# GpSimd's pattern shifts in six equivalent forms that take turns

## The chip, the cores and the metric

The kernel runs on one core of a Trainium2 chip. The metric is the device time of one execution in microseconds (us), lower is better. The engines are named as in the profile: PE is TensorE's matmul (PEld its weight load), ACT is ScalarE, DVE is VectorE, POOL is GpSimd, SP is SyncE. Each engine works through its own list of instructions in order; engines wait for each other on semaphores.

## The reference

Two attention blocks over a sequence of 2048 with width 512 and 32 heads of 16 channels, on separate inputs A and B. Their outputs stand side by side in `out` (2048 x 1024, bf16).

```python
# A: linear attention
pq, pk = phi(q), phi(k)          # phi(t) = (t + 1 if t > 0 else exp(t)) + 1e-6
o = (pq @ (pk^T v)) / (pq @ sum(pk) + 1e-6)      # per head
a = o @ wo
# B: softmax attention
scores = einsum("bhqd,bhkd->bhqk", q, k) * 16 ** -0.5
o = einsum("bhqk,bhkd->bhqd", softmax(scores), v)
b = o @ wo
return concatenate([a, b], axis=-1)
```

Nearly all of the time goes to B: 32 heads with a 2048 x 2048 table of exponentials each.

## The kernel before, in words

**Two ways to an exponential.** B is cut into 32 units: 4 groups of 8 heads, times 4 chunks of 512 queries, times the even or the odd heads of the group. A unit has 64 blocks: 16 key tiles of 128 for each of 4 heads. TensorE makes the scores of a block, 128 keys by 512 queries (line 871). Then the block goes one of two ways.

- On ScalarE: an exponential of two or three blocks at once, from PSUM to fp16 tiles in `PT` (line 1084). There are 648 of these.
- On VectorE and GpSimd: VectorE turns the scores into int16 numbers, `score * ESC + EB` (line 987). Read as fp16, such a bit pattern is a rough exponential (the linear interpolation between powers of two). To smooth the error, two more patterns are made from it by adding an integer: 328 and 656, the two entries of `SHIFT`. This is the "pattern shift". The three fp16 readings of one block all go into the weighted sum with V: the first through `VX` (V times the constant `VW`), the two shifted ones through `VV` (line 1253).

**The buffers.** `DI` holds 8 buffers (`NDG`) of up to two blocks (`DG`) each, in three versions: 0 the pattern, 1 shifted by 328, 2 shifted by 656. `di_at(v, b)` gives the place of version v of buffer b. A buffer comes free when TensorE has used all its versions.

**The shifts on GpSimd.** `chain` (line 1120) asks for both shifts when a buffer's patterns are complete. A shift normally goes to GpSimd (`on_pool`); version 2 goes to VectorE (`on_dve`, line 1141) where the planner's estimate of GpSimd's backlog is too long. Each buffer has one or two blocks, so a shift is 512 or 1024 elements wide in each of 128 partitions. Where two shifts wait together, `on_pool` joins them into one instruction over two buffers, twice as wide. Where one of the two is version 1 and the other version 2 ("mixed"), the second is made from version 1 by adding another 328, so one constant serves both. The instruction is the `tensor_scalar` at line 1176, with multiplication by 1.0 and then addition of the shift, int16 in and int16 out. There are 369 of them: 198 with 2048 elements a partition, 169 with 1024, 2 with 512.

**What sets the order.** A planner in the kernel's own host code simulates the engines with fixed durations, picks the next piece of work by due times and priorities (the table `SEG` changes these priorities every few us), and appends it to the engines' lists. It counts a GpSimd shift as 0.276 us and 0.83 ns an element. The order on each engine is therefore written out before the kernel runs and doesn't react to real durations; only the semaphore waits do. The planner counts the shift's duration, not its operations.

**Other work.** On GpSimd: zeros, ones and masks at the start (lines 485 to 522), `VX` from `VV` (line 684, `tensor_scalar` with two multiplications, bf16), and the normalisation of a unit's result (line 1288, `tensor_tensor`). Block A, the projections and the output products are jobs that the planner fills into TensorE and VectorE between the blocks of B.

Of the kernel before, what the change touches and what calls it, by code (L numbers as in the profile page):

```python
# [8 lines left out]
F32 = mybir.dt.float32  # L9
# [3 lines left out]
ALU = mybir.AluOpType  # L13
# [225 lines left out]
def bass_concat_heads__linear_attn_block__softmax_full_mha__prompt_kernel(nc, A_x, A_wqkv, A_wo, B_x, B_wqkv, B_wo, out):  # L239
# [19 lines left out]
    SHIFT = (328, 656)  # L259
# [98 lines left out]
    sch = Sched()  # L358
    es = contextlib.ExitStack()
    with es:  # L360
        block = es.enter_context(nc.Block())

        def sb(name, shape, dt):
            return es.enter_context(nc.sbuf_tensor(name, shape, dt))

        def ps(name, shape, dt):
            return es.enter_context(nc.psum_tensor(name, shape, dt))
# [12 lines left out]
        DI = sb("DI", [128, NDG * (32 + 2 * DGW + (DGW // 32) * 33 + 32)], I16)  # L380

        def di_at(v, b):

            if v == 0:
                return b * (32 + DGW) + 32
            if v == 1:
                return NDG * (32 + DGW) + b * DGW
            return NDG * (32 + 2 * DGW) + b * ((DGW // 32) * 33 + 32)
# [21 lines left out]
        TOP = sb("TOP", [128, 3], F32)  # L410
        TP1 = sb("TP1", [1, 4], F32)
        FLG = sb("FLG", [1, 1], F32)

        S5 = ps("pS", [128, 5 * 512], F32)
        SCR = [S5[:, 0:1024], S5[:, 1536:2560]]
# [18 lines left out]
        def gapped(ap, c0, n, run):  # L434

            base = ap[:, c0:c0 + run]
            return bass.AP(base.tensor, base.offset, [list(base.ap[0]), [run + 1, n], [1, run]])
# [70 lines left out]
        band(ZMk, 8, 1, "ZMk")  # L508
        sch.add("pool", lambda e: e.memset(DI[:, 0:NDG * (32 + DGW)].rearrange("p (b n) -> p b n", b=NDG)[:, :, 0:32], 0.0), writes=[("DI", 2, b_) for b_ in range(NDG)])
        sch.add("pool", lambda e: e.memset(EA[:, 512:528], 0.0), writes=["EA"])  # L510
        for e_ in range(2):
            sch.add("dve", lambda e, e_=e_: e.tensor_reduce(PAR[:, e_:e_ + 1], ZMk[:].rearrange("p (a e) -> p e a", e=2)[:, e_, :],
                                                           axis=AX.X, op=ALU.max),
                    reads=["ZMk"], writes=[("PAR", e_)])
# [24 lines left out]
        def push(eng, ready, prio, dur, run):  # L539
            seq[0] += 1  # L540
            c_ = (ready, prio, seq[0], dur, run)
            cands[eng].append(c_)
            return c_
# [32 lines left out]
        def f_op(lane, fn, reads=(), writes=()):  # L576
            return lambda bk: sch.add(lane, fn, reads=reads, writes=writes)
# [78 lines left out]
        def flag_job(**kw):  # L656
            def f(e, bk):
# [10 lines left out]
                ("pool", 0.15, f_op("pool", lambda e: e.tensor_tensor(TP1[:, 3:4], TP1[:, 3:4], TP1[:, 0:1], op=ALU.mult), ["TP1", "TP1b"], ["TP1b"])),  # L668
                ("pool", 0.15, f_op("pool", lambda e: e.tensor_tensor(FLG[:], TP1[:, 3:4], TP1[:, 2:3], op=ALU.mult), ["TP1", "TP1b"], ["FLG"]))],
                [("GRX", i) for i in range(4)] + [("TOP", 1), ("TOP", 2)], [], rel=2, **kw)  # L670
# [239 lines left out]
        def d_backlog(at):  # L910

            w = max(0.0, T["dve"] - at) + sum(c_[3] for c_ in cands["dve"])
            return w
# [206 lines left out]
        def chain(buf):  # L1120
            s_ = dgroup["st"][buf]
            if not s_["closed"] or len(s_["items"]) < s_["taken"]:
                return
            s_["chained"] = True
            late = left[NU - 1] < DE3 and all(b[0] == NU - 1 for b in s_["items"])
            n = len(s_["items"])
            w = 512 * n
            rk = [("DI", 0, buf, i) for i in range(n)]

            def give(buf_, v, lane, en_):  # L1130
                for i, b in enumerate(dgroup["st"][buf_]["items"]):
                    if lane == "dve":
                        P = gapped(DI.bitcast(F16), di_at(v, buf_) + 33 + i * 528, 16, 32)
                    else:
                        P = DI.bitcast(F16)[:, di_at(v, buf_) + i * 512:di_at(v, buf_) + (i + 1) * 512]
                    pv_ready[b[0]].append((en_ + (PM if lane == "pool" else LPE["dve"]), b, (P, ("DI", v, buf_)), ("d", buf_), "V"))

            def shift(v, t_):
                def on_dve(st_, en_):
                    wide = w + 32  # L1140
                    sch.add("dve", lambda e: e.tensor_scalar(gapped(DI, di_at(v, buf), wide // 32, 32), DI[:, di_at(0, buf) - 32:di_at(0, buf) + w], 1.0, float(SHIFT[v - 1]),  # L1141
                                                             op0=ALU.mult, op1=ALU.add), reads=rk, writes=[("DI", v, buf)])
                    give(buf, v, "dve", en_)

                def on_pool(st_, en_):
                    d1 = lambda b_: dgroup["st"][b_].get("v1", 1e9)
                    two = [x for x in pshift if x[2] == w and x[1] != buf and x[3][0] <= st_ + PMW
                           and (x[0] == v or d1(x[1] if v == 1 else buf) <= st_ + PMX)]
                    pshift.remove(me[0])
                    segs = [(buf, v)]  # L1150
                    keys = list(rk)
                    if two:
                        o = min(two, key=lambda x: (x[0] != v, x[3][2]))
                        pshift.remove(o)
                        cands["pool"].remove(o[3])
                        segs = sorted(segs + [(o[1], o[0])])
                        st_ = max(st_, o[3][0])
                        if o[0] != v:
                            st_ = max(st_, d1(o[1] if v == 1 else buf) - 0.03)
                            keys = []  # L1160
                            for b_, v_ in segs:
                                keys += [("DI", 1, b_)] if v_ == 2 else [("DI", 0, b_, i) for i in range(n)]
                        else:
                            keys += o[4]
                        T["pool"] = en_ = st_ + 0.276 + 2 * w * 0.00083
                    mixed = len({v_ for _, v_ in segs}) == 2
                    moves = sorted((di_at(1 if mixed and v_ == 2 else 0, b_), di_at(v_, b_)) for b_, v_ in segs)

                    def view(offs):
                        one = DI[:, offs[0]:offs[0] + w]  # L1170
                        if len(offs) == 1:
                            return one
                        return bass.AP(one.tensor, one.offset, [list(one.ap[0]), [offs[1] - offs[0], 2], [1, w]])
                    sv, dv = view([m_[0] for m_ in moves]), view([m_[1] for m_ in moves])
                    sh_ = float(SHIFT[0] if mixed else SHIFT[v - 1])
                    sch.add("pool", lambda e: e.tensor_scalar(dv, sv, 1.0, sh_, op0=ALU.mult, op1=ALU.add),  # L1176
                            reads=keys, writes=[("DI", v_, x) for x, v_ in segs])
                    for x, v_ in segs:
                        if v_ == 1:
                            dgroup["st"][x]["v1"] = en_  # L1180
                        pv_give[x, v_](en_)
                pv_give[buf, v] = lambda en_: give(buf, v, "pool", en_)
                if late:
                    def plain(st_, en_):
                        sch.add("dve", lambda e: e.tensor_scalar(DI[:, di_at(v, buf):di_at(v, buf) + w], DI[:, di_at(0, buf):di_at(0, buf) + w], 1.0, float(SHIFT[v - 1]), op0=ALU.mult, op1=ALU.add),
                                reads=rk, writes=[("DI", v, buf)])
                        give(buf, v, "plain", en_)
                    push("dve", t_, -2, 0.06 + w * 0.00027, plain)
                elif v == 2 and p_backlog(t_) - DSH * d_backlog(t_) > PSH:
                    push("dve", t_, 1, 0.06 + (w + 32) * 0.00053, on_dve)  # L1190
                else:
                    me = [(v, buf, w, push("pool", t_ + LAT + 0.05, 0, 0.276 + w * 0.00083, on_pool), rk)]
                    pshift.append(me[0])
            for v in (1, 2):
                shift(v, s_["t"])
# [178 lines left out]
        for t, bk, lane in ((2, SBANKS[1], "dve"), (3, SBANKS[2], "act")):  # L1374
            def tr(e, t=t, bk=bk):
# [6 lines left out]
                reads=[bk[3]], writes=[("xTb", t)])  # L1382
# [224 lines left out]

        flag_op = sch.last_write["FLG"]
        flag_op.sig = True
# [12 lines left out]
        def run(queue, e):  # L1622
            got = []
            def hook(e):
                e.wait_ge(sems[flag_op.lane], flag_op.count)
                got.append(e.value_load(FLG.bitcast(mybir.dt.int32)[0:1, 0:1], min_val=0))  # L1626
            sch.emit_queue(queue, e, sems, hook=(mark.idx - 1, hook))
# [54 lines left out]
```

## Time and profile before

| | |
|---|---|
| median of 2 runs | 661.57 us (661.22 to 661.92) |
| the profiled execution's own time | 660.98 us |
| its span in the trace | 659.2 us |
| mean granted TensorE clock | 0.999 |
| ScalarE busy | 644.7 us |
| TensorE busy | 633.3 us |
| VectorE busy | 632.1 us |
| GpSimd busy | 592.7 us, of it 554.4 us in the shifts of line 1176 |

How to read the lines that follow: a group's row names the line, the engine, the operation, output and inputs with their shapes, and the count; then the busy time in us and the mean of one in ns; then the idle time of that engine just before, and what ended most of it. A row of the waits gives the total in us, the number of waits and the longest. A row of the stretches gives, for each engine, the busy us and the number of instructions, then the granted clock, the share of the DMA engines and GB/s. A row of the order in time gives start, length, engine, line and the instructions joined in it. GpSimd's spans are rough.

### The profile page before, as it was taken

How to read it: one execution, taken by the hardware profiler on the slowest of the kernel's cores; microseconds unless marked ns; L12 is line 12 of the kernel's file. 1: busy time of each engine (PE TensorE's matmuls, PEld its weight loads, DVE VectorE, ACT ScalarE, POOL GpSimd, SP SyncE). 2: the span in 40 equal slices, each digit the busy share in tenths (PEclk: the TensorE clock that was granted, in tenths of full speed). 3: DMA queues.
4: the chain of work that ended last, by engine and by line, in shares of the span. 5: the costliest groups of instructions: out<-in, count | busy, mean ns of one | idle time of the engine just before them, and what ended most of it. 6: DMA issues, size and time to landing. Idle time of an engine off the chain costs nothing.

```text
span 659.2 us, 15950 instructions
## 1 busy us (share of the span) xinstructions
PE 633.3 (96%) x6609; PEld 200.4 (30%) x6662; DVE 632.1 (96%) x1089; ACT 644.7 (98%) x686; POOL 592.7 (90%) x450
## 2 busy tenths in 40 slices
PE   8999999999999999999999999999999999999997
PEld 6323333222333333332222233322222223232222
DVE  4999999999999999999999999999999999999995
ACT  6999999999999999999999999999999999999994
POOL 5999999999999999999998899999999999999983
PEclk9999999999999999999999999999999999999999
DMA  9701010020102101210012011010011000120102
GB/s 178 207 3 33 1 34 6 11 43 9 34 2 33 21 14 33 65 34 9 9 27 64 17 34 34 18 19 10 7 26 41 17 1 11 25 26 25 33 26 67
DMA packets 53213, 21.53 MB, mean 33 GB/s; under 512 B 44177, under 2 KB 52625, under 8 KB 53137
## 3 DMA queue, kind: packets, MB, share of 16 engines
q1 hardware_dynamic: 51664, 19.80, 13.9%
q8 instruction: 54, 0.88, 0.6%
q10 hardware_dynamic: 1472, 0.66, 0.4%
q14 instruction: 23, 0.18, 0.1%
HBM read 4.46 MB, written 4.19 MB: 13 GB/s over the span
## 4 chain that ended last, share of the span: by engine, by line
ACT 96%; PE 3%; DMA 1%; ACTq 0%; issue 0%; DVE 0%; DVEq 0%
ACT PT L1084 93%; ACT EA L693 2%; DMA Wb<-in_B_wqkv_dram 1%; PE pPV L1253 1%; PE pD L809 1%; PE pS L871 0%; PE pD L1305 0%; PE pS L1305 0%; PE pS L1389 0%; ACTq L442 0%; PE pD L1389 0%; DVE KNa L582 0%; PE pD L659 0%; PE pD L871 0%; DVEq L1626 0%
## 5 line engine op out<-in xcount | busy, mean ns | idle before, releaser
L1084 ACT ACTIVATE PT<-pS 128x1024 f16<-128x1024 f32 (+1 forms) x648 | 636.6, 1305 | 1.0 <-PE pS L871 1.0
L1176 POOL TENSOR_SCALAR DI<-DI 128x2048 int16<-128x2048 int16 (+1 forms) x369 | 554.4, 1503 | 47.3 <-DVE DI L987 20.2
L987 DVE TENSOR_SCALAR DI<-pD 128x512 int16<-128x512 f32 x492 | 324.4, 679 | 6.1 <-PE pD L871 2.5
L871 PE MATMUL pS<-QT,KM 32*128 32x512 bf16 x1556 | 255.0, 384 | 8.8 <-ACT PT L1084 4.5
L1253 PE MATMUL pPV<-PT,VV 128*17 128x512 f16 x1369 | 233.7, 381 | 0.0
L1253 PE MATMUL pPV<-DI,VV 128*17 128x512 f16 x1358 | 227.3, 382 | 0.0
L871 PE MATMUL pD<-QT,KM 32*128 32x512 bf16 x492 | 170.5, 384 | 0.3 <-DVE PQT L696 0.3
L1253 PE MATMUL pPV<-DI,VX 128*17 128x512 f16 x679 | 161.0, 381 | 0.2 <-DVE OT L1282 0.2
L871 PEld LDWEIGHTS pS<-QT,KM 32*128 32x128 bf16 x1556 | 64.6, 91 | 265.3 <-ACT PT L1084 227.4
L987 DVE TENSOR_SCALAR DI<-pS 128x512 int16<-128x512 f32 x187 | 126.6, 677 | 0.7
L1141 DVE TENSOR_SCALAR DI<-DI 128x1056 int16<-128x1056 int16 x113 | 77.0, 687 | 0.5
L1253 PEld LDWEIGHTS pPV<-PT,VV 128*17 128x17 bf16 x1369 | 47.5, 88 | 41.4 <-issue 36.1
L1253 PEld LDWEIGHTS pPV<-DI,VV 128*17 128x17 bf16 x1358 | 47.0, 88 | 40.4 <-issue 33.0
L871 PEld LDWEIGHTS pD<-QT,KM 32*128 32x128 bf16 x492 | 40.5, 91 | 5.4 <-DVE DI L987 2.0
L1253 PEld LDWEIGHTS pPV<-DI,VX 128*17 128x17 bf16 x679 | 34.2, 88 | 22.0 <-issue 17.7
L718 PE MATMUL pD<-Wa,xTa 128*128 128x256 bf16 x200 | 30.5, 275 | 0.3 <-DVE DI L987 0.2
L600 PE MATMUL pD<-xTb,Wb 128*128 128x512 bf16 x67 | 21.2, 383 | 3.1 <-issue 2.3
L1282 DVE STREAM_TRANSPOSE OT<-pPV 128x512 f32<-128x512 f32 x31 | 21.9, 705 | 0.1
L582 DVE CAST KNa<-pD 128x512 bf16<-128x512 f32 x27 | 18.4, 681 | 3.0 <-PE pD L809 2.0
L1288 POOL TENSOR_TENSOR OT<-OT,ZR 128x256 bf16<-128x256 f32 x31 | 19.3, 621 | 1.6
L718 PEld LDWEIGHTS pD<-Wa,xTa 128*128 128x128 bf16 x200 | 15.4, 97 | 13.3 <-issue 6.3
L693 ACT ACTIVATE EA<-pD 128x512 bf16<-128x512 f32 x23 | 19.2, 835 | 0.0
(136 smaller groups left out, 346.3 us busy)
## 6 DMA issues: line engine op xcount, KB each, us to landing
out_dram<-KNa SPq DMA_DIRECT2D x31, 128.0 KB, 1.7
Wa<-in_A_wqkv_dram SPq DMA_DIRECT2D x1, 1536.0 KB, 8.2
KM<-KR SPq DMA_DIRECT2D x96, 16.0 KB, 1.8
Wb<-in_B_wqkv_dram SPq DMA_DIRECT2D x2, 384.0 KB, 4.5
Wb<-in_B_wqkv_dram SPq DMA_DIRECT2D x1, 512.0 KB, 4.6
Wa<-in_A_wo_dram SPq DMA_DIRECT2D x1, 512.0 KB, 4.5
Wa<-in_B_wo_dram SPq DMA_DIRECT2D x1, 512.0 KB, 3.7
ON<-in_B_x_dram ACTq DMA_DIRECT2D x1, 256.0 KB, 3.1
```

Source lines behind the costliest of these rows:

```text
L582: return lambda e, bk: (e.tensor_copy(out_fn(), in_fn(bk)) if lane == "dve" else e.activation(out_fn(), in_fn(bk), ACTF.Copy))
L600: return e.matmul(f32v(bk), lhsT=Wb[:, cc, kind * 512 + Gp * 128:kind * 512 + Gp * 128 + 128], rhs=xTb[:, cc, sc * 512:(sc + 1) * 512], st ...
L693: ("act", 0.052 + n * 0.000833, f_ev("act", lambda e, bk: e.activation(EA[:, 0:n], f32v(bk)[:, c0:c0 + n], ACTF.Exp), [], ["EA"])),
L718: return e.matmul(f32v(bk)[:, 256 * tt:256 * tt + 256], lhsT=xTa[:, b, cc, (o + tt) * 128:(o + tt + 1) * 128], rhs=Wa[:, cc, 512 * kind + ...
L871: return e.matmul(dst, lhsT=KM[32 * g:32 * g + 32, Gp % 2, e_, j * 128:(j + 1) * 128], rhs=QT[32 * g:32 * g + 32, Gp % 2, c * 512:(c + 1) ...
L987: sch.add("dve", lambda e: e.tensor_scalar(DI[:, di_at(0, buf) + i * 512:di_at(0, buf) + (i + n) * 512], f32v(DBANK[b0], n * 512), ESC, EB ...
L1084: sch.add("act", lambda e: e.activation(PTf[:, p0 * 512:p0 * 512 + w], S5[:, c0:c0 + w], ACTF.Exp, scale=SC), reads=skeys(sl, len(bl)), wr ...
L1141: sch.add("dve", lambda e: e.tensor_scalar(gapped(DI, di_at(v, buf), wide // 32, 32), DI[:, di_at(0, buf) - 32:di_at(0, buf) + w], 1.0, fl ...
L1176: sch.add("pool", lambda e: e.tensor_scalar(dv, sv, 1.0, sh_, op0=ALU.mult, op1=ALU.add), reads=keys, writes=[("DI", v_, x) for x, v_ in s ...
L1253: sch.add("pe", lambda e, g=g, j=j, c0=c0, V_=V_, r2=r2, P=P, first=first, last_=last_: e.matmul(PVb[32 * g:32 * g + 17, 0:512] if len(P.s ...
L1282: sch.add("dve", lambda e: e.transpose(OT[:, 0, :], PVb[:, 0:512]), reads=[("PV", g) for g in range(4)], writes=[("OT", 0)])
L1288: ("pool", 0.7, f_op("pool", lambda e: e.tensor_tensor(xn[:, :, 16 * e_:16 * e_ + 16], o[:, :, 0:16], zr.unsqueeze(2).broadcast_to([128, 1 ...
```

## The change

Six ways to write the same shift take turns. A counter for each pair of constant (328 or 656) and number of buffers (one or two) picks the form, so each form gets close to a sixth of the instructions of each kind. The integers involved are exact in every form. Form 0 is the old instruction. Form 5 takes the constant from a new tile in SBUF, `SHC` (two columns of 128 partitions), which GpSimd fills with two memsets at the start, ahead of the zeros of `KM`. Operands, order, declared reads and writes and the planner's durations stay as they were.

```diff
+        SHC = sb("SHC", [128, 2], F32)
+        nform = defaultdict(int)
...
+        for v_ in range(2):
+            sch.add("pool", lambda e, v_=v_: e.memset(SHC[:, v_:v_ + 1], float(SHIFT[v_])), writes=["SHC"])
...
                     sh_ = float(SHIFT[0] if mixed else SHIFT[v - 1])
-                    sch.add("pool", lambda e: e.tensor_scalar(dv, sv, 1.0, sh_, op0=ALU.mult, op1=ALU.add),
-                            reads=keys, writes=[("DI", v_, x) for x, v_ in segs])
+                    kind_ = (sh_, len(segs))
+                    form = nform[kind_] % 6
+                    nform[kind_] += 1
+
+                    def op(e):
+                        if form == 0:
+                            return e.tensor_scalar(dv, sv, 1.0, sh_, op0=ALU.mult, op1=ALU.add)
+                        if form == 1:
+                            return e.tensor_scalar(dv, sv, sh_, 1.0, op0=ALU.add, op1=ALU.mult)
+                        if form == 2:
+                            return e.tensor_scalar(dv, sv, sh_, None, op0=ALU.add)
+                        if form == 3:
+                            return e.tensor_scalar(dv, sv, -sh_, None, op0=ALU.subtract)
+                        if form == 4:
+                            return e.tensor_scalar(dv, sv, sh_ / 2, sh_ / 2, op0=ALU.add, op1=ALU.add)
+                        return e.tensor_scalar(dv, sv, SHC[:, int(sh_ == SHIFT[1]):int(sh_ == SHIFT[1]) + 1], None, op0=ALU.add)
+                    sch.add("pool", op, reads=keys, writes=[("DI", v_, x) for x, v_ in segs])
```

## The prediction

> **What bounds the kernel now.** The profiled execution took 660.98 us, with a span of 659.2 us and some 1.7 us around it; it lies 0.6 us (0.1%) under the median of the runs shown, 661.57 us. All sums below are made against the profiled execution. I read the busy shares first, then the chain of work that ended last, then the costliest groups.
>
> ```profile
> PE 633.3 (96%) x6609; PEld 200.4 (30%) x6662; DVE 632.1 (96%) x1089; ACT 644.7 (98%) x686; POOL 592.7 (90%) x450
> ...
> ACT 96%; PE 3%; DMA 1%; ACTq 0%; issue 0%; DVE 0%; DVEq 0%
> ...
> L1084 ACT ACTIVATE PT<-pS 128x1024 f16<-128x1024 f32 (+1 forms) x648 | 636.6, 1305 | 1.0 <-PE pS L871 1.0
> L1176 POOL TENSOR_SCALAR DI<-DI 128x2048 int16<-128x2048 int16 (+1 forms) x369 | 554.4, 1503 | 47.3 <-DVE DI L987 20.2
> ```
>
> ScalarE bounds it: it makes 96% of the chain, and in front of its 648 exponentials it stood idle for 1.0 us in all. GpSimd is nowhere in the chain. Its busy share of 90% looks like 10% of room, and that is the figure to be careful with, because the edit touches 369 of its 450 instructions. So I went on to the stretches and to GpSimd's order in time.
>
> ```profile
> core 0: us, PE busy (x) PEld busy (x) DVE busy (x) ACT busy (x) POOL busy (x), PEclk, DMA share, GB/s
> 40.00:340.00 300.00, 292.45 (x3101) 94.05 (x3107) 294.57 (x509) 300.00 (x323) 277.38 (x201) 1.00 0.11 22
> 340.00:640.00 300.00, 289.38 (x3027) 84.13 (x3057) 295.60 (x502) 300.00 (x319) 276.72 (x192) 1.00 0.12 25
> sum 600.00, PE 581.83 PEld 178.18 DVE 590.17 ACT 600.00 POOL 554.10; mean PE 290.92 PEld 89.09 DVE 295.09 ACT 300.00 POOL 277.05
> ```
>
> ```profile
> 47.37 3.88 POOL L1176 TENSOR_SCALAR DI<-DI 128x2048 int16<-128x2048 int16 x2 [0.20 <-DVE DI L987]
> ...
> 319.85 2.17 POOL L1176 TENSOR_SCALAR DI<-DI 128x1024 int16<-128x1024 int16 x2
> ```
>
> ```profile
> POOL DI L1176 <- DVE DI L987: 20.2, 54, 1.0
> ...
> PEld pPV L1253 <- POOL DI L1176: 0.9, 4, 0.2
> ```
>
> ```profile
> L1176 POOL TENSOR_SCALAR DI<-DI 128x2048 int16<-128x2048 int16 x198 | 376.3, 1900 | 28.1 <-DVE DI L987 13.9 <-POOL DI L1176 2.0 <-DVE RD L770 0.2
> L1176 POOL TENSOR_SCALAR DI<-DI 128x1024 int16<-128x1024 int16 x169 | 176.9, 1047 | 18.2 <-DVE DI L987 6.3
> ...
> L1176 POOL TENSOR_SCALAR DI<-DI 128x512 int16<-128x512 int16 x2 | 1.2, 619 | 1.0 <-DVE TOP L662 0.9
> ```
>
> From 40 to 640 us GpSimd is busy for 554.1 of 600 us, over 393 instructions. Two shifts of 2048 that stand back to back take 3.88 us where their bodies make 3.80, and two of 1024 take 2.17 us where these make 2.09: each instruction occupies the engine for 0.08 us beyond its row. 393 of these are 31 us. So GpSimd is occupied for 585 of 600 us, and only about 15 us are free. The list of waits says the same: 20.2 us in 54 waits for VectorE's pattern, less 54 x 0.08, is 16 us. I take 16 us as GpSimd's real room. Nor is GpSimd late today: TensorE waited for a shifted pattern 4 times, 0.9 us in all.
>
> **The change part by part.**
>
> *The work.* Line 1176's `mult 1.0, add shift` is replaced by six forms in turn, counted apart for each shift constant and number of buffers, so each form gets nearly a sixth of each size. Nothing moves: order, operands, reads, writes and waits stay. What can change is the duration of 308 of the 369 shifts. Through the three sizes goes one straight line: (1900 - 1047) / 1024 = 0.833 ns an element and 1047 - 1024 x 0.833 = 194 ns fixed (512 elements by it: 621 ns, the row has 619). In all 198 x 2048 + 169 x 1024 + 2 x 512 = 579,584 elements a partition, hence 483 us by the element and 72 us fixed.
>
> *What a form can cost.* The trace has no one-operation form, no subtraction and no scalar from SBUF on GpSimd, so I bound them by what it has.
>
> ```profile
> L1288 POOL TENSOR_TENSOR OT<-OT,ZR 128x256 bf16<-128x256 f32 x31 | 19.3, 621 | 1.6
> L684 POOL TENSOR_SCALAR VX<-VV 128x544 bf16<-128x544 bf16 x16 | 10.3, 646 | 6.1 <-DVE VV L681 5.6
> L516 POOL MEMSET KM<- 128x512 bf16 x8 | 3.8, 528 | 0.0
> ...
> L504 POOL TENSOR_SCALAR_AFFINE_SELECT BMk<-BMk 128x128 bf16<-128x128 bf16 x1 | 0.3, 340 | 0.1
> ...
> L504 POOL TENSOR_SCALAR_AFFINE_SELECT ZMk<-ZMk 128x8 f32<-128x8 f32 x1 | 0.2, 193 | 0.1
> ...
> L667 POOL TENSOR_TENSOR TP<-TP 1x1 f32<-1x1 f32 x1 | 0.2, 183 | 0.3 <-DVE TP L665 0.3
> ...
> L510 POOL MEMSET EA<- 128x16 bf16 x1 | 0.1, 113 | 0.0
> L503 POOL MEMSET ZMk<- 128x8 f32 x1 | 0.1, 106 | 0.0
> ```
>
> Another pair of operations (mult, mult on bf16, line 684) runs on the same line: 194 + 544 x 0.833 = 647 ns, its row has 646. A memset does no arithmetic at all and reads nothing, and it too takes (528 - 113) / 496 = 0.837 ns an element. Zero operations and two operations, of two kinds and two types, cost the same by the element: the rate is that of moving elements, and arithmetic up to two operations hides in it. One operation lies between zero and two. So forms 1 to 4 are taken at 0.833 ns and 194 ns: no change. Against that speak two slower bodies: the affine select at (340 - 193) / 120 = 1.23 ns an element and the two-input multiply at (621 - 183) / 256 = 1.71 ns. Rate is thus not the same for all instructions; a one-operation body could be a different one. Below 0.833 ns no row goes, and a gain on GpSimd would not reach the end anyway: ScalarE is full in every stretch above. So the bounds by the element are 0.833 and 1.71 ns, and I take the lower because all rows of this very instruction lie on it.
>
> *Form 5, scalar from SBUF.* It is one operation and a further small read. An instruction that reads and writes 8 elements takes 193 ns, one that only writes them 106 ns: a read costs at most 0.09 us. The one-element multiply with two operand reads takes 183 ns, no more than the one-read select, so the lower end is 0. A sixth of 369, that is 62 instructions, gives 0 to 5.6 us; I take 3 us. It is hidden in the 16 us of room, except where a shift is consumed at once; I leave 0.5 us for that. Without that cover it costs the 3 us.
> [...]
>
> *Two memsets of SHC at the start*, ahead of GpSimd's zeroing of KM.
>
> ```profile
> 2.30 0.11 POOL L510 MEMSET EA<- 128x16 bf16 x1
> 2.35 3.80 POOL L516 MEMSET KM<- 128x512 bf16 x8
> ...
> 13.41 0.65 POOL L684 TENSOR_SCALAR VX<-VV 128x544 bf16<-128x544 bf16 x1 [4.45 <-DVE VV L681]
> ```
>
> The small memset at 2.30 us let the next start 0.05 us later, so two cost 0.1 to 0.2 us. GpSimd then stands idle for 4.45 us before 13.41 us, waiting for VectorE: hidden. Behind them in GpSimd's queue stand only zeros, ones and masks; without the cover it would be 0.2 us. The form counter is host work and costs nothing on the chip.
>
> *Sum.* 660.98 + 0 (forms 1 to 4) + 0.5 (form 5) + 0 (memsets) = 661.5 us.
>
> **The rivals.** A GpSimd that grows by X us costs nothing up to 16 us, and about X - 16 beyond it: the planner's order on all engines is fixed, so TensorE waits for the pattern, and ScalarE behind it. A shift that grows by 43 ns on average (16 us / 369) uses up the room; 2%, about what a measurement of this kernel can tell from no change, is 13.2 us more, so X = 29 us, or 79 ns on the average shift of 1503 ns. GpSimd becomes the bound sooner than its 90% tells.
>
> 1. *The one-operation forms (2, 3, 5) run a slower body.* Half of the elements, 241 us today. At the select's 1.23 ns they gain 241 x (1.23 / 0.833 - 1) = 115 us: 661 + 115 - 16 = 760 us. At the multiply's 1.71 ns it is 241 x 1.053 = 254 us: 899 us. For it: the trace holds two-operation forms alone, so the fast rate is shown for these only. Against it: the memset's rate. This is the rival on the other side; it decides from 0.833 + 0.12 ns an element on (29 us over half of the elements). Chance 0.27, of which 0.17 under 790 us.
> [...]
> 2. *Only form 5 is slow*, because the scalar is read like a second tensor: a sixth of the elements, 80.5 us, at 1.71 ns is 85 us more: 661 + 85 - 16 = 730 us. For it: the two-input row. Against it: a scalar is read once, not per element. Chance 0.08.
> 3. *Only the old pair of operations, or a few pairs, are quick*, and five forms are slow: 403 us x 0.477 at 1.23 ns is 192 us: 837 us. Against it: mult, mult is quick too. Chance 0.07.
> 4. *Small fixed costs on several forms*, 0.1 us on half of the shifts or more, with the room badly placed (back-to-back stretches have none): 18 to 37 us on GpSimd, 663 to 698 us. Chance 0.05 for more than 2%.
> 5. *Faster.* A one-operation form would need a rate under the memset's, and ScalarE would have to gain from it. Chance 0.01.
>
> **How the numbers follow.** The forecast, all forms alike, has 0.52; its own range is 658 to 668 us (the low end the runs' scatter and a slightly shorter fixed cost, the high end 5.6 us of form 5 unhidden). Slower by over 2%: 0.27 + 0.08 + 0.07 + 0.05 = 0.47. Faster by over 2%: 0.01. Within: 0.52. The range that holds 8 in 10 must take in rivals 2 and 4 and the milder part of rival 1: 0.52 + 0.08 + 0.05 + 0.17 = 0.82, up to 790 us. That is wide because one price, that of a one-operation shift, is in no row.
>
> **What would show each step.** In the profile after, GpSimd's rows of line 1176 and its new neighbours fall into groups by source line of each form: right if the 2048 groups all stand at 1.90 us and the 1024 groups at 1.05, form 5 up to 0.09 us above. TensorE's waits for DI from GpSimd stay near 1 us, and ScalarE keeps its 96% of the chain. Rival 1 would show as rows of 2.7 to 3.7 us for 2048 elements in forms 2, 3 and 5, GpSimd busy 97% or more, long waits of TensorE for shifted patterns, and GpSimd in the chain. What would make me wrong is the interpolation from zero and two operations to one.

## The result, and the profile after

| | before | after |
|---|---|---|
| median | 661.57 us (661.22 to 661.92) | 1364.34 us (1364.24 to 1364.44) |
| span of the profiled execution | 659.2 us | 1362.5 us |
| GpSimd busy | 592.7 us | 1320.4 us |
| ScalarE busy | 644.7 us | 687.6 us |

The changed kernel takes 2.062 times as long (95% interval 2.053 to 2.071). The forecast was no change; the range ended at 790 us. In the runs further down, one execution of e4 (871.7 us) and one of e10 (1008.0 us) stand far above the others of their kernel and are left out of the ratios; without it the median of e4 is 696.08 us, in place of the 696.76 us in its row.

The page of the changed kernel, its busy shares and the chain that ended last:

```profile
PE 888.6 (65%) x6609; PEld 233.3 (17%) x6662; DVE 659.2 (48%) x1089; ACT 687.6 (50%) x686; POOL 1320.4 (97%) x452
...
POOL 87%; PE 5%; issue 4%; DVE 3%; DMA 0%; ACTq 0%; DVEq 0%; POOLq 0%
POOL DI L1194 24%; POOL DI L1192 18%; POOL DI L1190 17%; POOL DI L1195 16%; POOL DI L1188 5%; POOL DI L1186 5%; DVE DI L991 2%; PE pPV L1272 2%; PE pS L875 1%; POOL OT L1307 1%; POOL VX L688 1%; PE pD L681 0%; DMA Wb<-in_B_wqkv_dram 0%; PE pD L604 0%; PE pD L813 0%
```

Read the chain first: ScalarE had 96% of it and is gone from it, GpSimd has 87%. Four lines make three quarters of it, and two lines of the same instruction make 5% each. The lines are the forms: 1186 is form 0 (mult, add), 1188 form 1 (add, mult), 1190 form 2 (add), 1192 form 3 (subtract), 1194 form 4 (add, add), 1195 form 5 (add from SBUF). Here are GpSimd's groups by shape in the changed kernel; after the count stand busy us and mean ns:

```profile
L1194 POOL TENSOR_SCALAR DI<-DI 128x2048 int16<-128x2048 int16 x33 | 234.0, 7095 | 1.7 <-DVE DI L991 0.7 <-POOL DI L1192 0.2 <-POOL DI L1194 0.2
L1192 POOL TENSOR_SCALAR DI<-DI 128x2048 int16<-128x2048 int16 x33 | 177.1, 5367 | 1.1
L1190 POOL TENSOR_SCALAR DI<-DI 128x2048 int16<-128x2048 int16 x33 | 177.0, 5365 | 2.8 <-DVE DI L991 1.2 <-POOL DI L1188 0.5 <-POOL DI L1194 0.2
L1195 POOL TENSOR_SCALAR DI<-DI,SHC 128x2048 int16<-128x2048 int16 x32 | 174.0, 5439 | 1.2 <-POOL DI L1194 0.3 <-POOL DI L1188 0.2
L1194 POOL TENSOR_SCALAR DI<-DI 128x1024 int16<-128x1024 int16 x28 | 101.7, 3639 | 0.8
...
L1190 POOL TENSOR_SCALAR DI<-DI 128x1024 int16<-128x1024 int16 x28 | 77.5, 2769 | 0.8 <-DVE DI L991 0.2
L1195 POOL TENSOR_SCALAR DI<-DI,SHC 128x1024 int16<-128x1024 int16 x27 | 76.8, 2845 | 0.9
L1186 POOL TENSOR_SCALAR DI<-DI 128x2048 int16<-128x2048 int16 x34 | 64.5, 1897 | 3.8 <-DVE DI L991 1.1 <-POOL DI L1194 0.2 <-POOL DI L1195 0.2
L1188 POOL TENSOR_SCALAR DI<-DI 128x2048 int16<-128x2048 int16 x33 | 62.6, 1897 | 2.8 <-POOL DI L1186 0.3 <-POOL DI L1195 0.3
```

Forms 0 and 1 kept the old 1.90 us. Two sizes of each form give its price by the element: forms 2 and 3, (5365 - 2769) / 1024 = 2.54 ns; form 5, (5439 - 2845) / 1024 = 2.53 ns; form 4, (7095 - 3639) / 1024 = 3.38 ns. These are close to 3, 3 and 4 times the 0.833 ns of the old pair. Nearly all of the growth is there: 33 x 3.47 + 28 x 1.72 = 163 us for form 2 and the same for form 3, 162 us for form 5, 33 x 5.20 + 28 x 2.59 = 244 us for form 4, 731 us in all. GpSimd's busy time grew by 728 us and the span by 703 us; where the 24 us between them went is told at the end of the experiments.

The list of waits shows how this reaches the end:

```profile
ACT PT L1088 <- PE pD L875: 376.2, 195, 9.8
...
PEld pPV L1272 <- POOL DI L1194: 187.5, 50, 7.1
PE pPV L1272 <- POOL DI L1194: 162.6, 50, 6.8
```

TensorE waits up to 7.1 us at a time for a shifted pattern. Its order is written out, so the scores that ScalarE needs stand behind that wait, and ScalarE waits for TensorE. ScalarE's own work grew by only 43 us; it was starved.

### The profile page after: what moved, and what is told of

Its sections match the earlier page's. It is cut to its first block, busy times and chain, and to the rows that moved or that the text cites. A ratio compares the mean times of both kernels' runs of the same rounds, so it can differ in the third digit from the quotient of the medians.

```text
span 1362.5 us, 15952 instructions
## 1 busy us (share of the span) xinstructions
PE 888.6 (65%) x6609; PEld 233.3 (17%) x6662; DVE 659.2 (48%) x1089; ACT 687.6 (50%) x686; POOL 1320.4 (97%) x452
## 4 chain that ended last, share of the span: by engine, by line
POOL 87%; PE 5%; issue 4%; DVE 3%; DMA 0%; ACTq 0%; DVEq 0%; POOLq 0%
POOL DI L1194 24%; POOL DI L1192 18%; POOL DI L1190 17%; POOL DI L1195 16%; POOL DI L1188 5%; POOL DI L1186 5%; DVE DI L991 2%; PE pPV L1272 2%; PE pS L875 1%; POOL OT L1307 1%; POOL VX L688 1%; PE pD L681 0%; DMA Wb<-in_B_wqkv_dram 0%; PE pD L604 0%; PE pD L813 0%
## 5 line engine op out<-in xcount | busy, mean ns | idle before, releaser
L1088 ACT ACTIVATE PT<-pS 128x1024 f16<-128x1024 f32 (+1 forms) x648 | 671.0, 1081 | 659.3 <-PE pD L875 376.2
L1272 PE MATMUL pPV<-DI,VV 128*17 128x512 f16 x1358 | 330.4, 484 | 426.5 <-POOL DI L1194 162.6
L1194 POOL TENSOR_SCALAR DI<-DI 128x2048 int16<-128x2048 int16 (+1 forms) x61 | 335.6, 5508 | 2.5 <-DVE DI L991 0.7
L1272 PE MATMUL pPV<-PT,VV 128*17 128x512 f16 x1369 | 333.3, 480 | 0.0
L875 PE MATMUL pS<-QT,KM 32*128 32x512 bf16 x1556 | 321.1, 485 | 5.9 <-DVE DI L991 3.9
L1190 POOL TENSOR_SCALAR DI<-DI 128x2048 int16<-128x2048 int16 (+2 forms) x62 | 255.7, 4130 | 4.6 <-DVE DI L991 1.4
L1192 POOL TENSOR_SCALAR DI<-DI 128x2048 int16<-128x2048 int16 (+1 forms) x61 | 254.5, 4176 | 1.6
L1195 POOL TENSOR_SCALAR DI<-DI,SHC 128x2048 int16<-128x2048 int16 (+2 forms) x60 | 252.3, 4207 | 2.1 <-POOL DI L1194 0.3
L875 PE MATMUL pD<-QT,KM 32*128 32x512 bf16 x492 | 213.0, 482 | 16.4 <-DVE DI L991 8.9
L1272 PE MATMUL pPV<-DI,VX 128*17 128x512 f16 x679 | 209.5, 472 | 2.0 <-POOL VX L688 1.7
L1186 POOL TENSOR_SCALAR DI<-DI 128x2048 int16<-128x2048 int16 (+1 forms) x63 | 94.8, 1505 | 6.4 <-DVE DI L991 1.6
L1188 POOL TENSOR_SCALAR DI<-DI 128x2048 int16<-128x2048 int16 (+1 forms) x62 | 92.9, 1498 | 5.0 <-POOL DI L1186 0.3
L722 PE MATMUL pD<-Wa,xTa 128*128 128x256 bf16 x200 | 41.0, 344 | 0.0
```

The source lines that it names most:

```text
L722: return e.matmul(f32v(bk)[:, 256 * tt:256 * tt + 256], lhsT=xTa[:, b, cc, (o + tt) * 128:(o + tt + 1) * 128], rhs=Wa[:, cc, 512 * kind + ...
L875: return e.matmul(dst, lhsT=KM[32 * g:32 * g + 32, Gp % 2, e_, j * 128:(j + 1) * 128], rhs=QT[32 * g:32 * g + 32, Gp % 2, c * 512:(c + 1) ...
L1088: sch.add("act", lambda e: e.activation(PTf[:, p0 * 512:p0 * 512 + w], S5[:, c0:c0 + w], ACTF.Exp, scale=SC), reads=skeys(sl, len(bl)), wr ...
L1186: return e.tensor_scalar(dv, sv, 1.0, sh_, op0=ALU.mult, op1=ALU.add)
L1188: return e.tensor_scalar(dv, sv, sh_, 1.0, op0=ALU.add, op1=ALU.mult)
L1190: return e.tensor_scalar(dv, sv, sh_, None, op0=ALU.add)
```

## The experiments

Theory A: GpSimd has a fast body for pairs of operations that hold a multiplication and a slow general one for the rest. Theory B: a form is slow because forms take turns. Further rivals were the conversion of int16 (A2), and that a multiplication by 1.0 is dropped (A3). A second question was how much of GpSimd's growth is hidden: the prediction gave it 16 us of room.

**One fast form alone, and one slow form alone.**

```diff
-  e.tensor_scalar(dv, sv, 1.0, sh_, op0=ALU.mult, op1=ALU.add)
+  e.tensor_scalar(dv, sv, sh_, 1.0, op0=ALU.add, op1=ALU.mult)    # e1_add_mult
+  e.tensor_scalar(dv, sv, sh_, None, op0=ALU.add)                 # e2_add_alone
```

> All 369 shifts in form 1 (add the shift, then multiply by 1.0), nothing else changed. Theory A (GpSimd has a fast body for pairs that hold a multiplication, 0.833 ns an element, and a general body for the rest, about two cycles an element and one more for each operation: 2.53 ns for one, 3.38 ns for two): rows of 1897 and 1044 ns as in the changed kernel, 661 to 663 us. Theory B (a form is slow because forms alternate, so that each instruction finds another form's code before it): also fast, since nothing alternates, 661 to 663 us. A theory by which the order of the operations matters would give more.

> All 369 shifts in form 2 (one addition), nothing alternates. Theory A: 198 x 5.365 + 169 x 2.770 + 2 x 1.49 = 1533 us in the shifts, 979 us more than before; with some 24 us of it absorbed, as in the changed kernel, 1590 to 1640 us. Theory B: 1.90 and 1.05 us again, 661 to 665 us.

Measured: e1 660.97 us, a ratio of 0.9997 (0.9987 to 1.0007). e2 1584.91 us, a ratio of 2.397 (2.392 to 2.402). The cycles in which the expectation of e1 counts are the author's estimate from the rows of the changed kernel (3.38 - 2.53 = 0.85 ns an element for the second addition, close to the 0.833 of the old pair); no run shows a clock of GpSimd. GpSimd's groups in e2:

```profile
L1176 POOL TENSOR_SCALAR DI<-DI 128x2048 int16<-128x2048 int16 x198 | 1059.3, 5366 | 4.9 <-POOL DI L1176 3.2
L1176 POOL TENSOR_SCALAR DI<-DI 128x1024 int16<-128x1024 int16 x169 | 465.6, 2771 | 1.4 <-DVE DI L987 0.6
```

Nothing takes turns here, and one addition takes 5366 and 2771 ns, as it did among the other forms. Theory B falls. The time ended 5 us under the range that was written down: more was absorbed than the 24 us of the changed kernel (the end of this section says by what).

**A price list.** Behind GpSimd's last instruction of the kernel before stand forms on a scratch tile, each with 1024 and with 512 elements, each on its own line. The output is computed as before; the time has the list in it and is not compared.

```diff
+        def price(fn):
+            for n_ in (1024, 512):
+                sch.add("pool", lambda e, n_=n_: fn(e, n_), reads=[], writes=allk)
+        price(lambda e, n: e.tensor_scalar(TB[:, 0:n], TA[:, 0:n], 1.0, 328.0, op0=ALU.mult, op1=ALU.add))
+        price(lambda e, n: e.tensor_scalar(TB[:, 0:n], TA[:, 0:n], 328.0, None, op0=ALU.add))
...
```

> The kernel before, and behind its last instruction on GpSimd a list of tensor_scalar forms on a scratch tile, each with 1024 and 512 elements, alone on the chip. The output is that of the reference; the time is longer by the list and says nothing. Theory A by the element: mult with add, mult with mult, mult with subtract and subtract with mult 0.83 ns; add alone 2.53; add with add and add with subtract 3.38; max with add 3.4; mult alone is the open one (0.83 if any multiplication takes the fast body, 2.53 if only pairs do). A rival, A2 (the conversion of int16 makes the general body slow): add alone on bf16 and fp32 0.83 ns, where theory A has 2.5 for these too. A second rival, A3 (one of the two operations must be an addition or a multiplication by 1.0 that is dropped): mult 1.0 alone fast, mult 2.0 alone slow.

Rows of e3 with 1024 elements. Lines: 1624 mult, subtract; 1625 subtract, mult; 1627 add, add; 1629 max, add; 1619 add; 1633 mult on bf16; 1622 mult by 1.0; 1634 add on fp32; 1636 two-input add; 1621 mult, add with both scalars from SBUF; 1616 mult, add; 1623 mult, mult; 1630 copy.

```profile
L1625 POOL TENSOR_SCALAR DI<-DI 128x1024 int16<-128x1024 int16 x1 | 3.6, 3639 | 0.1
...
L1627 POOL TENSOR_SCALAR DI<-DI 128x1024 int16<-128x1024 int16 x1 | 3.6, 3639 | 0.1
L1624 POOL TENSOR_SCALAR DI<-DI 128x1024 int16<-128x1024 int16 x1 | 3.6, 3634 | 0.1
L1629 POOL TENSOR_SCALAR DI<-DI 128x1024 int16<-128x1024 int16 x1 | 3.6, 3634 | 0.1
...
L1619 POOL TENSOR_SCALAR DI<-DI 128x1024 int16<-128x1024 int16 x1 | 2.8, 2785 | 0.1
L1633 POOL TENSOR_SCALAR DI<-DI 128x1024 bf16<-128x1024 bf16 x1 | 2.8, 2777 | 0.1
...
L1622 POOL TENSOR_SCALAR DI<-DI 128x1024 int16<-128x1024 int16 x1 | 2.8, 2774 | 0.1
L1634 POOL TENSOR_SCALAR DI<-DI 128x1024 f32<-128x1024 f32 x1 | 2.8, 2772 | 0.1
...
L1636 POOL TENSOR_TENSOR DI<-DI 128x1024 bf16<-128x1024 bf16 x1 | 1.9, 1891 | 0.1
...
L1621 POOL TENSOR_SCALAR DI<-DI,SHC 128x1024 int16<-128x1024 int16 x1 | 1.2, 1188 | 0.1
L1616 POOL TENSOR_SCALAR DI<-DI 128x1024 int16<-128x1024 int16 x1 | 1.0, 1044 | 0.1
...
L1623 POOL TENSOR_SCALAR DI<-DI 128x1024 int16<-128x1024 int16 x1 | 1.0, 1043 | 0.1
...
L1630 POOL COPY DI<-DI 128x1024 int16<-128x1024 int16 x1 | 1.0, 1036 | 0.1
```

A2 falls: one addition takes 2.77 to 2.79 us on int16 and fp32 alike. Theory A as written falls too: mult with subtract (3634 ns) and subtract with mult (3639) are pairs that hold a multiplication, and they are slow. A multiplication alone, which theory A left open, is slow as well (2774). Left as fast are the copy and the pairs mult-add and mult-mult (add-mult by e1). Call that theory A'. What still had to be told apart was whether the 1.0 in these pairs is what makes them fast.

**A second list, without a 1.0.** Made like the first, with the constants 1.5, 2.5 and 3.0 on bf16.

```diff
+        price(lambda e, n: e.tensor_scalar(BB[:, 0:n], BA[:, 0:n], 1.5, 3.0, op0=ALU.mult, op1=ALU.add))
+        price(lambda e, n: e.tensor_scalar(BB[:, 0:n], BA[:, 0:n], 3.0, 1.5, op0=ALU.add, op1=ALU.mult))
+        price(lambda e, n: e.tensor_scalar(BB[:, 0:n], BA[:, 0:n], 1.5, 2.5, op0=ALU.mult, op1=ALU.mult))
...
```

> A second list of forms behind the end of the kernel before, on a scratch tile, 1024 and 512 elements; the output stays that of the reference. Theory A' (the fast body belongs to the pairs mult-add, add-mult and mult-mult): 1.5 with 3.0 in these three pairs 0.83 ns an element; add-add, max-min, mult-max 3.35; max alone and subtract alone 2.5. Rival A3 (a pair is fast since one of its operations is a multiplication by 1.0 and is dropped): the three pairs with 1.5, 2.5 and 3.0 are slow too, 3.35, and so is nothing else changed. Conversion int16 to fp32 and bf16 to fp32: 0.83 if the type costs nothing.

Rows of e8: 1615 mult, add; 1616 add, mult; 1617 mult, mult; 1618 add, add; 1619 max, min; 1620 mult, max; 1621 max; 1622 subtract; 1623 mult, add from int16 to fp32.

```profile
L1618 POOL TENSOR_SCALAR DI<-DI 128x1024 bf16<-128x1024 bf16 x1 | 3.7, 3659 | 0.1
L1620 POOL TENSOR_SCALAR DI<-DI 128x1024 bf16<-128x1024 bf16 x1 | 3.6, 3641 | 0.1
...
L1621 POOL TENSOR_SCALAR DI<-DI 128x1024 bf16<-128x1024 bf16 x1 | 2.8, 2777 | 0.1
L1622 POOL TENSOR_SCALAR DI<-DI 128x1024 bf16<-128x1024 bf16 x1 | 2.8, 2774 | 0.1
...
L1615 POOL TENSOR_SCALAR DI<-DI 128x1024 bf16<-128x1024 bf16 x1 | 1.0, 1047 | 0.1
L1617 POOL TENSOR_SCALAR DI<-DI 128x1024 bf16<-128x1024 bf16 x1 | 1.0, 1047 | 0.1
L1623 POOL TENSOR_SCALAR DI<-DI 128x1024 f32<-128x1024 int16 x1 | 1.0, 1047 | 0.1
L1616 POOL TENSOR_SCALAR DI<-DI 128x1024 bf16<-128x1024 bf16 x1 | 1.0, 1046 | 0.1
```

A3 falls: without a 1.0 the same three pairs are fast. A' holds for all forms tried, which are not all pairs that could be written; what in the engine makes these three quick, no run shows.

**The changed kernel with one form undone, and with all repaired.**

```diff
-  return e.tensor_scalar(dv, sv, sh_ / 2, sh_ / 2, op0=ALU.add, op1=ALU.add)
+  return e.tensor_scalar(dv, sv, sh_, 1.0, op0=ALU.add, op1=ALU.mult)                              # e9, form 4 alone
...
-  return e.tensor_scalar(dv, sv, sh_, None, op0=ALU.add)
+  return e.tensor_scalar(dv, sv, sh_, 1.0, op0=ALU.add, op1=ALU.mult)                              # e10, form 2
-  return e.tensor_scalar(dv, sv, -sh_, None, op0=ALU.subtract)
+  return e.tensor_scalar(dv, sv, sh_, 1.0, op0=ALU.add, op1=ALU.mult)                              # e10, form 3
-  return e.tensor_scalar(dv, sv, sh_ / 2, sh_ / 2, op0=ALU.add, op1=ALU.add)
+  return e.tensor_scalar(dv, sv, 1.0, sh_, op0=ALU.mult, op1=ALU.add)                              # e10, form 4
-  return e.tensor_scalar(dv, sv, SHC[:, int(sh_ == SHIFT[1]):int(sh_ == SHIFT[1]) + 1], None, op0=ALU.add)
+  return e.tensor_scalar(dv, sv, SHC[:, int(sh_ == SHIFT[1]):int(sh_ == SHIFT[1]) + 1], SHC[:, 2:3], op0=ALU.add, op1=ALU.mult)   # e10, form 5
```

> The changed kernel with form 4 alone undone: in place of add-add it adds the shift and multiplies by 1.0. By the rows of the changed kernel form 4 takes 7.10 us for 2048 elements (33 of them) and 3.64 for 1024 (28), where the fast body with its gap takes 1.98 and 1.12: 33 x 5.1 + 28 x 2.5 = 238 us. If GpSimd is the bound and the forms' prices simply add, 1364 - 238 = 1120 to 1135 us. If part of the growth is due to something else (the lower TensorE clock, other waits), the time comes out higher or lower than that by its share.

> The changed kernel with all its six forms still taking turns, but each a pair with a multiplication: forms 2 and 3 add the shift and multiply by 1.0, form 4 multiplies by 1.0 and adds, form 5 adds and multiplies with both scalars from SBUF. Theory A' (the pair of operations decides, nothing else of the change costs anything): 661 to 663 us. Theory B (taking turns between forms costs something): clearly above 665 us.

Measured: e9 1126.07 us (1.7035 times the kernel before, 1.7001 to 1.7069), where 1364 - 238 is 1126. e10 661.18 us, a ratio of 1.000 (0.999 to 1.001). Six lines in turn, now of three fast forms, with a tile of constants and its three memsets, cost nothing; which operations a shift is written with is the whole effect.

**How much of a growth is hidden.** Two doses of long shifts and two of slightly longer ones.

```diff
+  npool[0] += 1
+  slow = npool[0] % 24 == 0        # e4; % 6 in e5: one addition instead of the pair
...
+  ptr = npool[0] % 3 == 0          # e6; every shift in e7: the pair mult, add with both scalars from SBUF
```

> The old form, but every 24th shift is one addition: 15 slow shifts, each 3.47 us longer at 2048 elements or 1.73 at 1024, some 39 us more on GpSimd in all, spread over the whole run. If 16 us of room on GpSimd hide what comes first (the prediction's step): 661 + 39 - 16 = 680 to 688 us. If each slow shift is paid in full, since TensorE needs its pattern at once: 698 to 702 us. If the queue of patterns ready ahead hides single late shifts: 661 to 668 us. TensorE's granted clock should stay above 0.95.

> The old form, but every sixth shift is one addition: 61 slow shifts, about 61 x 2.6 = 160 us more on GpSimd. Paid nearly in full: 661 + 160 less 5 to 20 us = 800 to 815 us. With a granted clock between that of the 15 slow shifts (0.98) and that of the changed kernel (0.72). If a lower TensorE clock cost time by itself, it would lie above 821 us.

> The old pair (multiply by 1.0, add the shift), but in every third shift both scalars come from SBUF. By the price list (762 and 1188 ns against 617 and 1044) this is 0.145 us more for 123 shifts, 18 us on GpSimd, in small even steps. Theory R16 (GpSimd's 16 us of waits are room for such a growth, as the prediction had it): 661 to 664 us. Theory R0 (what GpSimd grows by is paid nearly in full, since its waits come from the same loop that it slows): 675 to 680 us. In between, as with the 15 long shifts, where 36 of 40 us were paid: 670 to 677 us.

> Both scalars from SBUF in all 369 shifts: 53 us more on GpSimd. Theory R16: 661 + 53 - 16 = 694 to 700 us. Theory R0: 711 to 716 us. TensorE's clock near full speed in either.

| kernel | median us | ratio (95%) | GpSimd busy, growth | GpSimd's waits (33 us before) | span, growth |
|---|---|---|---|---|---|
| e6, 123 shifts a little longer | 661.64 | 1.0009 (1.0000 to 1.0018) | 16.9 us | 21 us | 0.7 us |
| e7, 369 shifts a little longer | 669.22 | 1.0125 (1.0109 to 1.0140) | 47.9 us | 16 us | 7.4 us |
| e4, 15 shifts much longer | 696.76 | 1.0538 (1.0517 to 1.0559) | 38.7 us | 26 us | 32.5 us |
| e5, 61 shifts much longer | 824.99 | 1.2480 (1.2457 to 1.2503) | 167.9 us | 27 us | 162.9 us |
| e9, 183 shifts much longer | 1126.07 | 1.7035 (1.7001 to 1.7069) | 485.4 us | 18 us | 465.4 us |
| e2, all much longer | 1584.91 | 2.3971 (2.3923 to 2.4019) | 967.6 us | 12 us | 923.7 us |

The waits are the sum of GpSimd's list of waits, that is, of its idle stretches of more than 0.15 us. What a growth takes from them is hidden.

e7 came out far under both theories, and the rows say why. In e7 two and more shifts back to back:

```profile
106.42 3.55 POOL L1183 TENSOR_SCALAR DI<-DI,SHC 128x1024 int16<-128x1024 int16 x3
...
L1183 POOL TENSOR_SCALAR DI<-DI,SHC 128x1024 int16<-128x1024 int16 x169 | 200.6, 1195 | 1.8 <-DVE DI L991 1.6
```

Three take 3.55 us where three rows make 3.59: the gap of 0.08 us between shifts is gone. From start to start one takes (3.55 - 1.195) / 2 = 1.18 us, against 2.17 - 1.047 = 1.12 us before: 0.055 us more, not 0.148 as the rows say. Over 369 shifts that is 20 us, of which 8 were paid and 12 hidden. GpSimd's waits for VectorE's pattern had been 20.2 us. In e7 they are these:

```profile
POOL DI L1183 <- DVE DI L991: 3.7, 12, 0.8
```

All its waits together fell by 17 us, with 43 fewer of them; each of those held a gap of 0.08 us too, which leaves some 14 us. In e6 the two kinds of shift stand mixed and this spacing doesn't price them, but the waits fell by 12 us (10 by the same count) and 0.5 us were paid. So some 12 to 14 of the 16 us of room are real for a growth spread evenly. For 15 long shifts they are not: of about 39 us, e4 paid 32 in the profiled execution and some 35 in the median, which lies between the ranges written down for 16 us of room (680 to 688 us) and for none (698 to 702 us). Its waits for VectorE's pattern still add up to 13 us, and TensorE waited for the slow line and for the fast one behind it:

```profile
PEld pPV L1257 <- POOL DI L1180: 14.2, 29, 2.0
POOL DI L1180 <- DVE DI L987: 12.9, 36, 0.8
...
PEld pPV L1257 <- POOL DI L1179: 10.6, 6, 2.5
```

These rows fit the reading that the room lies scattered in short waits: a shift that is 3.5 us longer uses up those near it, and the others stay unused. No run varied the spacing alone.

e5 ended 10 us above its range, which counted 160 us for the slow shifts. They are 36 of 2048 elements and 25 of 1024, so 36 x 3.47 + 25 x 1.72 = 168 us, paid nearly in full.

In e2, 44 us of the busy growth are not in the span, and in the changed kernel 24. The waits fell by 21 and by 15 us. The rest are gaps between rows that closed, as in e7. Here are three slow shifts of e2:

```profile
365.56 8.24 POOL L1176 TENSOR_SCALAR DI<-DI 128x1024 int16<-128x1024 int16 x3
```

From start to start one takes (8.24 - 2.77) / 2 = 2.74 us, a little less than its row of 2.77, where the old pair takes 0.08 us more than its row.

## Why the prediction was wrong

The step that failed: "One operation lies between zero and two. So forms 1 to 4 are taken at 0.833 ns and 194 ns: no change." That is an interpolation over a quantity, the number of operations, that does not set the price. Form 1 did stay at the old price. Forms 2 and 3, with fewer operations, took 2.54 ns an element, form 4, with as many as the old pair, 3.38. What sets the price is which operations are paired. That the rate is one of moving elements, in which arithmetic hides, was the author's inference from two pairs and a memset; no run shows it, and the 2.50 to 2.54 ns of one operation speak against it.

- *The bounds failed too.* The upper end, 1.71 ns from the two-input multiply, was a row of another instruction. It does not bound this one: the price list has the two-input add at (1891 - 1037) / 512 = 1.67 ns, under every slow tensor_scalar. The second fast row on which the step leaned, mult-mult of line 684, is one of the three fast pairs; the trace before held no `tensor_scalar` outside them.
- *Rival 1 had a slower body at the wrong price, rival 3 the right scope.* Rival 1 bounded one operation at 1.23 to 1.71 ns where 2.54 was measured, and left form 4 among the fast ones. Its threshold of 0.12 ns an element is a slip: 29 us over half of 579,584 elements is 0.10. "Only the old pair of operations, or a few pairs, are quick" is what the runs show, with four slow forms instead of five. Rival 3 was given 0.07 and argued down with the very row that shares the fast price.
- *Form 5's scalar* was bounded at 0 to 0.09 us. Against form 2 it costs 5439 - 5365 = 74 ns and 2845 - 2769 = 76 ns a row: inside, and alike at both sizes, where rival 2 had it grow by the element.
- *The memsets* were hidden, as e10 shows (three of them, a ratio of 1.000).
- *The sum rule was right in size.* X - 16 gives 661 + 728 - 16 = 1373 us for the measured growth, 0.6% over. With the price known, the forecast would have been good. The 16 us stand close to the 15 us by which the waits fell; the other 9 us, of gaps that closed, the rule didn't have. For few long shifts (e4) it would have been 12 us too low (661 + 39 - 16 = 684 us).
- *GpSimd's 90% as nearly full* was right: it is why a slower shift shows almost in full, 703 of 728 us.

## What to carry to other kernels

A cheap-looking simplification on GpSimd can cost three to four times by the element, 2.54 and 3.38 ns against 0.833 in the changed kernel: here `tensor_scalar` with one addition took 2.65 times as long at 1024 elements (2771 ns in e2) as the same addition paired with a multiplication by 1.0 (1047 ns before), so write adds and scalings there as mult-add, add-mult or mult-mult (1043 to 1047 ns). When an edit puts in a form that the trace does not hold, rows of other instructions are no bounds; measure each form on a scratch tile behind the kernel's end, at two sizes, before trusting a price. Where an engine is full once its gaps are counted, a small even growth can be hidden in its waits and gaps, while a few long instructions are paid nearly in full: here the span took 0.7 of 16.9 us in e6 and 7.4 of 47.9 in e7, but 32.5 of 38.7 in e4.

## What was not expected of the hardware

Prices by the element on GpSimd, from the two sizes in e3, e8 and the changed kernel, stand near whole multiples of the 0.834 ns of a copy ((1036 - 609) / 512): 1 for the three pairs (0.83 ns), 2 for a two-input add (1.67 ns), 3 for one operation of any kind tried (2.50 to 2.54), 4 for any other pair tried (3.34 to 3.39). Operand type made a difference of under 1% in the forms measured on more than one: mult-add (1044 ns) and one addition (2772 to 2785) on int16, bf16 and fp32, add-add (3639 and 3659) on int16 and bf16.

TensorE's granted clock was lower the less of the span TensorE was busy: 1.00 at 96% before, 0.98 at 95% in e4, 0.93 at 85% in e5, 0.80 at 74% in e9, 0.72 at 65% in the changed kernel, 0.67 at 62% in e2. From the changed kernel to e9 it rose from 0.72 to 0.80, and the time fell by just the price of form 4, so no cost of the clock shows there. e5 lies 4 us above the 821 us that were written down for a clock without a cost, but that bound had the 160 us in it; with 168 it is 829 us, and e5 lies under it. No run shows a cost of the lower clock.
